# Two pairs of first-layer tiles by seven products on the half blocks, laced with plain tiles

## The chip, the cores and the metric

The kernel runs on one NeuronCore of a Trainium2 chip. The metric is the device time of one execution in microseconds; 655.01 us is the median of three runs before the change. One of the executions was taken by the hardware profiler, and all profile lines come from that one.

The engines named below are PE (TensorE, matrix products; PEld is its weight load), DVE (VectorE), ACT (ScalarE), POOL (GpSimd) and SP (SyncE, which here only issues DMAs). Each works through its own queue in order. PE writes to PSUM[...].

## The reference

A gated linear attention over 768 steps with complex gates, for 32 heads of 48 channels, followed by a two-layer network with the gate h cos(h):

```python
for t in range(S):
    ar, ai = (a_re_n[:, :, t, :, None], a_im_n[:, :, t, :, None])
    new_re = ar * S_re - ai * S_im
    new_im = ar * S_im + ai * S_re
    kv = np.einsum('bhd,bhe->bhde', k[:, :, t], v[:, :, t])
    S_re, S_im = (new_re + kv, new_im)
    y[:, :, t] = np.einsum('bhd,bhde->bhe', q[:, :, t], S_re)
...
h = x @ w_in
g = h * np.cos(h)
return (g @ w_out).astype(np.float32)
```

`x` has 3072 rows (tokens) of 384; `w_in` is 384 x 2048 and `w_out` 2048 x 384. All is fp32.

## The kernel before

The 3072 tokens are cut into 24 chunks of 128, and two chunks make a group: 12 groups, 0 to 11. For each group the kernel computes the logs and phases of the gates (`log_steps`, `p_powers` with PSUM tile `lgs`, `g_phase` with `phs`), scales keys and queries by them (`g_stack`: tiles `ks`, `qs`), turns both (`f_transpose`: a DVE transpose into tile `tr`, a DMA to a buffer `moved` in DRAM, DMAs back as `kT` and `qT`), multiplies scores (`sc`, masked by DVE into `atm`), adds values and the carried state (`yp`, `sp`), and sends the result through DRAM into `xT` (`f_x`, `f_xt`), the transposed input of the network.

The first layer takes `xT`, 3 blocks of 128 channels x 2 chunks of 128 tokens. It makes the 2048 hidden columns in 8 tiles jp = 0 to 7 of 256 columns each. One tile fills one PSUM bank `hp` with 2 x 3 products of 128 weight columns and 256 tokens (`mm1_sums`, line 1061). Then ACT writes the cosine to `gate` and squares `hp` into a scratch tile with a running sum (`gate_sine`), and DVE multiplies (`gate_product`). A product in fp32 leaves two matmul records in the profile, each with its weight load.

The second layer of groups 2 to 11 already works by seven products instead of eight on half blocks: `mixed` (line 1140) forms sums and differences of gate tiles in tiles `s`, `quarters` and `last_quarter` those of `w_out`, and `seventh` multiplies them into the tiles `sum` and `op`.

Groups 0, 1 and the first steps of 2 are ordered by hand. From group 2 on, a loop at line 1568 laces the work. Pass n holds the second layer of group n-1, the attention of group n, the gates and keys of group n+1, and from 0.56 of its length the first layer of group n (`first`). The function `weave` (line 1213) sorts the pieces by the fractions written beside them. The products on PE are chained in just that order. On DVE, ACT and SP the framework's scheduler lays the pieces out by what is ready; each engine then keeps that order. Every operation of DVE and many of ACT are recorded at line 676, all products at 687, so tiles tell them apart.

The parts of a pass that matter here, in PE's order: scores and values of group n, among them second-layer products of group n-1; the `lgs` products for group n+1; more second-layer products; the `phs` products; the last 16 records of the second layer; then the whole first layer. `keys(n+1)` (trigonometry, `g_stack`, `p_end`, both `f_transpose`) runs on DVE and ACT at the start of that first layer. `p_end` reads the tile `end`, the last row of P, which `even_steps` sends out and back through DRAM (`row_out`, `row_back`, lines 833 and 838).

PSUM is split into two pools: `pa`, five banks under one name for attention work, and `pm`, three banks for `hp`, `op` and `sum`.

```python
              (phases(n + 1), *((0.472, 0.476) if n == PLAIN else (0.516, 0.524))),
              (keys(n + 1), *((0.5, 0.62) if n == PLAIN else (0.53, 0.64))),
              (last_quarter() if n == PLAIN else [], 0.9, 1.0), (first(n), 0.56, 1.0),
```

Of the kernel before, what the change touches and what calls it, by code (L numbers as in the profile page):

```python
# [11 lines left out]
F32 = mybir.dt.float32  # L12
# [475 lines left out]
def fast_path(ctx, tc, q, k, v, a_re, a_im, moe_w_in, moe_w_out, out, least, odd, wide,  # L488
# [323 lines left out]
    def even_steps(g, i, n):  # L812
# [16 lines left out]
        if g > 0:  # L829
            row_out(g, i, n, nc.sync)  # L830
            row_back(g, i, n, nc.sync)

    def row_out(g, i, n, queue):
        P = cut(X[g]["P"], i, n)
        queue.dma_start(out=X[g]["row"][ds(i * DM, n * DM)],
                        in_=P[C - 1:C].rearrange("o x -> (o x)"))
# [215 lines left out]
    def f_xt(g, i=0, n=G):  # L1052

        if i == 0:
            X[g]["xT"] = msb.tile([C, ND, G, C], F32, tag="xT", name="xT")
        moved = X[g]["moved"].rearrange("p s d g t -> (p s d) g t").rearrange("(c r) g t -> r c g t", r=C)
        put = nc.sync.dma_start(out=X[g]["xT"][:, :, ds(i, n)], in_=moved[:, :, ds(i, n)])
        behind(put, late["x"])
        late["x"] = put
# [18 lines left out]

    def gate_sine(g, jp):
        x = X[g]  # L1080
        ps = x["hp"][jp]
        gate = x["gate"][jp] = msb.tile([C, 2, G * C], F32, tag="gate", name="gate", bufs=8)
        junk = msb.tile([C, 2, G * C], BF16, tag="junk", name="junk", bufs=1)
        special(out=gate, in_=ps, func=AF.Sin, scale=1.0 / in_scale, bias=half_pi_b)
# [3 lines left out]
    def gate_product(g, jp):  # L1088
        x = X[g]
        gate = x["gate"][jp]  # L1090
        gated = vector.tensor_tensor(out=gate, in0=x["hp"].pop(jp), in1=gate, op=ALU.mult)
        x.setdefault("gated", gated)

    def mm1_gate(g, jp):
        gate_sine(g, jp)
        gate_product(g, jp)

# [4 lines left out]
    def mm2(g, i, j0, nj):  # L1102
# [7 lines left out]
        if j0 + nj == NJ:  # L1110
            ot = msb.tile([C, DM], F32, tag="ot", name="ot")
            scalar.mul(out=ot, in_=ps, mul=1.0 / (in_scale * out_scale))
            nc.sync.dma_start(out=out[ts(g * G + i, C), :], in_=ot)
# [26 lines left out]
    def mixed(g, p):  # L1140
# [3 lines left out]
        s = stage["pool"].tile([C, 3, 2, C], F32, tag="s", name="s", bufs=HJ // 2)  # L1144
        s1, s2, s4 = (s[:, i] for i in range(3))
# [14 lines left out]
    def seventh(g, p, part):  # L1160
# [34 lines left out]
        elif p == 4:  # L1195
            put = nc.sync.dma_start(out=out[ds(row + C, C), :], in_=x["ot"][1])
            if g == NG - 1:
                behind(put, late["read SP"])
# [61 lines left out]
    def chunks(g):  # L1260
# [6 lines left out]
        if g + 2 < NG:  # L1267
            yield lambda: load(g + 2, ("k", "q", "v"))

    def first(g):  # L1270
        order = range(NJ // 2) if g < PLAIN else (0, 4, 1, 5, 2, 6, 3, 7)
# [296 lines left out]
    for n in range(2, NG):  # L1568
        weave((mixes(n - 1, 2, 4), 0.0, 0.12), (logs(n + 1), 0.0, 0.02), (chunks(n), 0.0, 0.36),
              (upper[2:] if n == 2 else [], 0.0, 0.2), (products(n - 1, 0, 2 + (n < NG - 1)), 0.0, 0.36),  # L1570
              (prods(n + 1), 0.25, 0.27), (second(n - 1, 1), 0.36, 0.5),
              (products(n - 1, 2 + (n < NG - 1), 7), 0.4, 0.56),
              (phases(n + 1), *((0.472, 0.476) if n == PLAIN else (0.516, 0.524))),
              (keys(n + 1), *((0.5, 0.62) if n == PLAIN else (0.53, 0.64))),
              (last_quarter() if n == PLAIN else [], 0.9, 1.0), (first(n), 0.56, 1.0),
# [102 lines left out]
```

## Time and profile before

| | |
|---|---|
| median of three runs | 655.01 us (654.78 to 655.53) |
| the profiled execution | 653.01 us |
| its span, first to last instruction | 651.2 us |
| matmul records, PE | 4075 |
| of them `hp` of 256 columns | 1128, 246.5 us |
| of them `hp` of 128 columns | 48, 6.0 us |
| ACT `gate<-hp` and DVE `gate<-hp`, each | 96 x 0.69 us |
| DVE transposes `tr<-ks` and `tr<-qs` | 20 x 2.25 us |
| first layer of one group, from first to last `hp` | 20.72 us |

The first layers of groups 3 to 11, the ones that the change touches, start at 204.16, 255.37, 305.61, 355.93, 407.14, 457.37, 507.69, 559.38 and 607.45 us. The page names the time by engines and groups of instructions; a stage is best read from the windows view (busy time of each engine between two moments) with the timelines of the engines beside it. Matmuls overlap in their records: the mean of one `hp` record is 379 ns, but the next starts 216 ns after it. Start-to-start is the price; the rest is drain.

### The profile page before, as it was taken

Reading aid. Unit: us, or ns where it says so; the run is one execution under the profiler, and the core shown is the slowest. Engines: PE = TensorE matmul, PEld = TensorE weight load, DVE = VectorE, ACT = ScalarE, POOL = GpSimd, SP = SyncE. Lnnn points to the kernel's source line nnn. Section 1 sums busy time; section 2 is a strip of 40 time slices with the busy share of each in tenths; the row PEclk is TensorE's granted clock in tenths of the full one; section 3 lists DMA queues with packets and bytes.
Section 4 is the critical chain, followed back from the end, with each engine's and each line's share of the span. In section 5 each row is a group of like instructions: output and inputs, shape, how many; then the busy total and the mean of one; then the engine's idle time right before and its main releaser. Section 6 shows DMA issues by size and latency. Waiting matters only on the chain.

```text
span 651.2 us, 10758 instructions
## 1 busy us (share of the span) xinstructions
PE 641.0 (98%) x4075; PEld 576.4 (89%) x4075; DVE 492.0 (76%) x799; ACT 392.8 (60%) x726; POOL 30.9 (5%) x53
## 2 busy tenths in 40 slices
PE   8999999999999999999999999999999999999997
PEld 6888877777999999899899899899899999999996
DVE  6999989888687688786787787876877878862251
ACT  7898687284583593494494485485576476433330
POOL 4010200000000000010010010000000000000000
PEclk9999999999999999999999999999999999999999
DMA  9968755727627656747738737836836843363001
GB/s 249 244 179 203 225 164 123 170 62 182 146 49 182 158 146 148 194 110 167 209 82 191 204 85 167 205 96 151 226 105 146 219 123 98 112 134 120 25 1 31
DMA packets 232920, 94.90 MB, mean 146 GB/s; under 512 B 208701, under 2 KB 221246, under 8 KB 232858
## 3 DMA queue, kind: packets, MB, share of 16 engines
q1 hardware_dynamic: 225320, 68.51, 45.3%
q0 software_dynamic: 5824, 25.50, 11.7%
q8 instruction: 34, 0.56, 0.4%
q10 hardware_dynamic: 1714, 0.11, 0.2%
q14 instruction: 28, 0.23, 0.1%
HBM read 69.28 MB, written 24.81 MB: 144 GB/s over the span
## 4 chain that ended last, share of the span: by engine, by line
PE 92%; ACT 4%; DVE 3%; DMA 0%; issue 0%; SPq 0%; DVEq 0%
PE hp L687 38%; PE op L687 18%; PE sum L687 16%; PE sc L687 6%; PE yp L687 6%; PE sp L687 4%; PE phs L687 2%; PE lgs L687 1%; ACT tan L707 1%; PE yr L687 1%; PE tp L948 1%; ACT rs L707 1%; ACT lg L707 1%; ACT L703 1%; DVE mag L676 1%; DVE atm L676 1%
## 5 line engine op out<-in xcount | busy, mean ns | idle before, releaser
L687 PE MATMUL hp<-xT,w_in 128*128 128x256 f32 (+1 forms) x1176 | 252.5, 375 | 0.0
L687 PEld LDWEIGHTS hp<-xT,w_in 128*128 128x128 f32 x1176 | 219.6, 190 | 30.2 <-issue 0.2
L707 ACT ACTIVATE gate<-hp,half_pi_b 128x512 f32<-128x512 f32 x96 | 66.0, 687 | 118.5 <-PE hp L687 118.5
L687 PE MATMUL op<-w_out,gate 128*128 128x192 f32 (+1 forms) x448 | 100.7, 374 | 0.0
L676 DVE TENSOR_TENSOR gate<-hp,gate 128x512 f32<-128x512 f32 x96 | 65.7, 684 | 45.8 <-ACT junk L676 45.7
L687 PEld LDWEIGHTS op<-w_out,gate 128*128 128x128 f32 x448 | 75.9, 190 | 16.9 <-issue 2.0
L676 ACT ACTIVATE junk<-hp 128x512 bf16<-128x512 f32 x96 | 56.7, 591 | 0.0
L687 PE MATMUL sum<-t_s,s 128*128 128x192 f32 x320 | 56.3, 329 | 0.0
L687 PEld LDWEIGHTS sum<-t_s,s 128*128 128x128 f32 x320 | 52.1, 190 | 1.5 <-issue 1.5
L676 DVE TENSOR_TENSOR atm<-sc,causal 128x512 f32<-128x512 f32 x48 | 32.9, 689 | 23.4 <-PE sc L687 23.4
L687 PEld LDWEIGHTS sc<-qT,kT 96*128 96x128 f32 x384 | 47.4, 192 | 2.3 <-issue 0.6
L687 PE MATMUL sc<-qT,kT 96*128 96x128 f32 x384 | 49.0, 276 | 0.2 <-ACT qT L676 0.2
L676 ACT ACTIVATE ot<-sum 128x192 f32<-128x192 f32 x39 | 12.6, 322 | 53.7 <-PE sum L687 53.4
L676 DVE SCALAR_TENSOR_TENSOR ot<-op,ot 128x192 f32<-128x192 f32 x40 | 13.3, 354 | 38.0 <-PE op L687 36.4
L687 PE MATMUL yp<-atm,v 128*48 128x128 f32 x352 | 33.6, 277 | 0.9 <-ACT Q L707 0.6
L703 ACT ACT_TABLE_LOAD x24 | 30.8, 1283 | 1.2 <-PEq L1662 0.7
L676 ACT COPY yT<-yp 48x512 f32<-48x512 f32 x44 | 25.3, 574 | 7.4 <-PE yp L687 7.0
L687 PE MATMUL yp<-qT,state 96*48 96x128 f32 x304 | 29.7, 272 | 0.0
L687 PE MATMUL sum<-w_out,gate 128*128 128x192 f32 x160 | 29.7, 329 | 0.0
L687 PE MATMUL sp<-v,ks 128*96 128x48 f32 x320 | 29.7, 245 | 0.0
L687 PEld LDWEIGHTS sp<-v,ks 128*96 128x96 f32 x320 | 29.6, 165 | 0.0
L676 ACT CAST tan<-phs 128x384 int32<-128x384 f32 x24 | 11.4, 480 | 29.4 <-PE phs L687 29.4
(147 smaller groups left out, 987.4 us busy)
## 6 DMA issues: line engine op xcount, KB each, us to landing
moved<-tr SPq DMA_DIRECT2D x20, 768.0 KB
raw<-in_moe_w_in_dram POOLq DMA_DIRECT2D x16, 768.0 KB, 5.1
raw<-in_moe_w_out_dram POOLq DMA_DIRECT2D x16, 768.0 KB, 4.6
kT<-moved SPq DMA_DIRECT2D x40, 192.0 KB
qT<-moved SPq DMA_DIRECT2D x10, 768.0 KB
k<-in_k_dram SPq DMA_DIRECT2D x24, 192.0 KB
q<-in_q_dram SPq DMA_DIRECT2D x24, 192.0 KB
v<-in_v_dram SPq DMA_DIRECT2D x24, 192.0 KB
```

The costliest lines, as they stand in the source:

```text
L676: ins = getattr(self.engine, op)(**kw)
L687: chain(nc.tensor.matmul(out, **kw), "tensor")
L703: chain(nc.scalar.preload_act_table_set(table))
L707: chain(nc.scalar.activation(func=func, **kw))
L948: chain(nc.tensor.transpose(ps[:, h], X[g][name[0] + "s"][:, x0 + h].rearrange("p a d -> p (a d)"), ident), "tensor")
```

## The change

It changes four of the eight tiles of the first layer in groups 3 to 11. Tiles jp and jp+4 with jp = 0 and jp = 2 form a pair; the two tiles, two chunks of tokens and the first two of the three channel blocks make a 2 x 2 by 2 x 2 block product, done by seven products on mixed blocks; the third channel block is added plainly. Counted in matmul records, a pair takes 44 records of 128 tokens (22 products with 128 weight columns each) instead of 24 records of 256 tokens (12 products).

- `halves_mixed` forms the mixed weights once (three new blocks of 256 columns for each pair, and one in place in `w_in`), on DVE; `x_mixed` forms five mixed blocks of `xT` for each group, on DVE.
- `in_sevens(g, b, step)` does one pair in four steps. Both tiles of the pair live in banks of pool `pa`, two regions of 256 columns in each: "11" and "12" in the upper tile's bank, "21" and "22" in the lower one's. Region "12" carries the running sum; it is copied three times by ACT into the gate tiles (`kept`), and DVE adds the copies into the other regions.
- `first` runs the pairs' steps with the plain tiles 1, 5, 3, 7 between them.
- The mixed gates `s` of the second layer get no tiles of their own but buffers of `qs` and `tr`.
- The write of the last row of P and its two reads (`ends`) become a piece of their own at 0.36 of the pass, and on SP they, the loads of k, q, v and the stores of the output stand behind the write of `xT`.

On PE the 96 records of a group's first layer become 136. Nothing else on PE moves.

```diff
--- before.py
+++ after.py
@@ -826,14 +826,19 @@
         for one_, what in zip(ins, ("carried", "split")):
             if what in x and g > PEG:
                 behind(one_, x[what])
-        if g > 0:
-            row_out(g, i, n, nc.sync)
-            row_back(g, i, n, nc.sync)
+        if 0 < g <= PLAIN:
+            ends(g)
+
+    def ends(g):
+        put = row_out(g, 0, G, nc.sync)
+        if g > PLAIN:
+            behind(put, X[g - 1]["back"])
+        row_back(g, 0, G, nc.sync)
 
     def row_out(g, i, n, queue):
         P = cut(X[g]["P"], i, n)
-        queue.dma_start(out=X[g]["row"][ds(i * DM, n * DM)],
-                        in_=P[C - 1:C].rearrange("o x -> (o x)"))
+        return queue.dma_start(out=X[g]["row"][ds(i * DM, n * DM)],
+                               in_=P[C - 1:C].rearrange("o x -> (o x)"))
 
     def row_back(g, i, n, queue):
         row = X[g]["row"][ds(i * DM, n * DM)]
@@ -1056,7 +1061,7 @@
         moved = X[g]["moved"].rearrange("p s d g t -> (p s d) g t").rearrange("(c r) g t -> r c g t", r=C)
         put = nc.sync.dma_start(out=X[g]["xT"][:, :, ds(i, n)], in_=moved[:, :, ds(i, n)])
         behind(put, late["x"])
-        late["x"] = put
+        late["x"] = X[g]["back"] = put
 
     def mm1_sums(g, jp, i=None):
 
@@ -1076,24 +1081,111 @@
                        rhs=x["xT"][:, dc, ds(lo, n)].rearrange("p g t -> p (g t)"),
                        start=(dc == 0), stop=(dc == ND - 1))
 
+    def alike(*tiles):
+
+        if len(tiles[-1].shape) == 3:
+            return tiles
+        return [t.rearrange("p j (i c) -> p j i c", i=G) for t in tiles[:-1]] + [
+            tiles[-1].rearrange("p i j c -> p j i c")]
+
     def gate_sine(g, jp):
         x = X[g]
         ps = x["hp"][jp]
-        gate = x["gate"][jp] = msb.tile([C, 2, G * C], F32, tag="gate", name="gate", bufs=8)
+        if jp not in x["gate"]:
+            x["gate"][jp] = msb.tile([C, 2, G * C], F32, tag="gate", name="gate", bufs=8)
+        gate = x["gate"][jp]
         junk = msb.tile([C, 2, G * C], BF16, tag="junk", name="junk", bufs=1)
+        gate, junk, ps = alike(gate, junk, ps)
         special(out=gate, in_=ps, func=AF.Sin, scale=1.0 / in_scale, bias=half_pi_b)
         scalar.activation(out=junk, in_=ps, func=AF.Square, scale=1.0 / in_scale,
                           accum_out=wide[:, ds(g * (NJ // 2) + jp, 1)])
 
     def gate_product(g, jp):
         x = X[g]
-        gate = x["gate"][jp]
-        gated = vector.tensor_tensor(out=gate, in0=x["hp"].pop(jp), in1=gate, op=ALU.mult)
+        gate, ps = alike(x["gate"][jp], x["hp"].pop(jp))
+        gated = vector.tensor_tensor(out=gate, in0=ps, in1=gate, op=ALU.mult)
         x.setdefault("gated", gated)
 
     def mm1_gate(g, jp):
         gate_sine(g, jp)
         gate_product(g, jp)
+
+    SEVENS, PARTED = 3, (0, 2)
+    parted = {}
+
+    def halves_mixed():
+
+        for b in PARTED:
+            t = parted[b] = stage["pool"].tile([C, 3, W], F32, name=f"w_mix{b}")
+            a11, a12, a21, a22 = (w_in[:, r * (NJ // 4) + b, c] for r in range(2) for c in range(2))
+            yield lambda t=t, a=a21, b_=a22: vector.scalar_tensor_tensor(
+                out=t[:, 0], in0=a, scalar=-1.0, in1=b_, op0=ALU.mult, op1=ALU.subtract)
+            yield lambda t=t, a=a11: vector.scalar_tensor_tensor(
+                out=t[:, 1], in0=t[:, 0], scalar=-1.0, in1=a, op0=ALU.mult, op1=ALU.subtract)
+            yield lambda t=t, a=a12: vector.tensor_tensor(
+                out=t[:, 2], in0=a, in1=t[:, 1], op=ALU.subtract)
+            yield lambda a=a11, b_=a21: vector.tensor_tensor(out=b_, in0=a, in1=b_, op=ALU.subtract)
+
+    def x_mixed(g):
+
+        xT = X[g]["xT"]
+        t = X[g]["xm"] = stage["pool"].tile([C, 5, C], F32, tag="xm", name="xm", bufs=1)
+        b12, b21, b22 = xT[:, 0, 1], xT[:, 1, 0], xT[:, 1, 1]
+        vector.tensor_tensor(out=t[:, 0:2], in0=xT[:, 0::2, 0], in1=xT[:, 0::2, 1], op=ALU.subtract)
+        vector.tensor_tensor(out=t[:, 2], in0=b22, in1=t[:, 0], op=ALU.add)
+        vector.tensor_tensor(out=t[:, 3], in0=b22, in1=b12, op=ALU.subtract)
+        vector.tensor_tensor(out=t[:, 4], in0=b21, in1=t[:, 2], op=ALU.subtract)
+
+    def in_sevens(g, b, step):
+
+        x, up, low = X[g], b, b + NJ // 4
+        if step == 0:
+            for jp in up, low:
+                x.setdefault("hp", {})[jp] = pa.tile([C, G, 2, C], F32, tag="a", name="hp")
+                x.setdefault("gate", {})[jp] = msb.tile([C, 2, G * C], F32, tag="gate",
+                                                        name="gate", bufs=8)
+        xT, xm, mix = x["xT"], x["xm"], parted[b]
+        place = {"11": (up, 0), "12": (up, 1), "21": (low, 0), "22": (low, 1)}
+
+        def at(c):
+            jp, i = place[c]
+            return x["hp"][jp][:, i]
+
+        def kept(c):
+            jp, i = place[c]
+            return x["gate"][jp][:, :, ds(i * C, C)]
+
+        def product(c, a, moving, fresh=False):
+            for ji in range(2):
+                matmul(at(c)[:, ji], lhsT=a[:, ts(ji, C)], rhs=moving,
+                       start=fresh and ji == 0, stop=True, skip_group_check=True)
+
+        def add(c, a):
+            vector.tensor_tensor(out=at(c), in0=at(a), in1=kept(c), op=ALU.add)
+
+        if step == 0:
+            product("12", w_in[:, up, 0], xT[:, 0, 0], True)
+            scalar.copy(out=kept("11"), in_=at("12"))
+            product("11", w_in[:, up, 1], xT[:, 1, 0])
+            product("11", w_in[:, up, 2], xT[:, 2, 0])
+            add("11", "11")
+        elif step == 1:
+            product("12", mix[:, 1], xm[:, 2])
+            scalar.copy(out=kept("21"), in_=at("12"))
+            product("21", w_in[:, low, 0], xm[:, 3], True)
+            product("21", w_in[:, low, 2], xT[:, 2, 1])
+        elif step == 2:
+            product("12", mix[:, 0], xm[:, 0])
+            scalar.copy(out=kept("22"), in_=at("12"))
+            add("22", "21")
+        else:
+            product("12", mix[:, 2], xT[:, 1, 1])
+            product("12", w_in[:, up, 2], xT[:, 2, 1])
+            mm1_gate(g, up)
+            product("21", w_in[:, low, 1], xm[:, 4])
+            product("21", w_in[:, low, 2], xm[:, 1])
+            add("21", "21")
+            mm1_gate(g, low)
 
     def mm1(g, jp):
         mm1_sums(g, jp)
@@ -1110,7 +1202,9 @@
         if j0 + nj == NJ:
             ot = msb.tile([C, DM], F32, tag="ot", name="ot")
             scalar.mul(out=ot, in_=ps, mul=1.0 / (in_scale * out_scale))
-            nc.sync.dma_start(out=out[ts(g * G + i, C), :], in_=ot)
+            put = nc.sync.dma_start(out=out[ts(g * G + i, C), :], in_=ot)
+            if g > 0 and i > 0:
+                behind(put, X[g + 1]["back"])
 
 
 
@@ -1141,8 +1235,10 @@
 
         lo, hi = X[g]["gate"][p], X[g]["gate"][p + HJ // 2]
         a11, a21, a12, a22 = lo[:, :, 0:C], lo[:, :, C:2 * C], hi[:, :, 0:C], hi[:, :, C:2 * C]
-        s = stage["pool"].tile([C, 3, 2, C], F32, tag="s", name="s", bufs=HJ // 2)
-        s1, s2, s4 = (s[:, i] for i in range(3))
+        if p % 2 == 0:
+            pool, tag = ((gt, "qs"), (ft, "tr"))[p // 2]
+            X[g]["s"] = pool.tile([C, 2, 3, 2, C], F32, tag=tag, name="s")
+        s1, s2, s4 = (X[g]["s"][:, p % 2, i] for i in range(3))
         for out_, a, b, op in ((s1, a21, a22, ALU.add), (s2, s1, a11, ALU.subtract),
                                (a21, a11, a21, ALU.subtract), (s4, a12, s2, ALU.subtract)):
             vector.tensor_tensor(out=out_, in0=a, in1=b, op=op)
@@ -1194,8 +1290,7 @@
             behind(nc.sync.dma_start(out=out[ds(row, C), 0:E2], in_=c11), late["line"])
         elif p == 4:
             put = nc.sync.dma_start(out=out[ds(row + C, C), :], in_=x["ot"][1])
-            if g == NG - 1:
-                behind(put, late["read SP"])
+            behind(put, late["read SP"] if g == NG - 1 else X[g + 1]["back"])
         elif p == 6 and alone:
             late["store"] = lambda: nc.scalar.dma_start(out=out[ds(row, C), E2:DM], in_=c12)
         elif p == 6:
@@ -1265,9 +1360,15 @@
             yield lambda n=n: f_out(n)
         yield lambda: (f_x(g), f_xt(g))
         if g + 2 < NG:
-            yield lambda: load(g + 2, ("k", "q", "v"))
+            yield lambda: load(g + 2, ("k", "q", "v"), put=lambda **kw: behind(
+                nc.sync.dma_start(**kw), X[g]["back"]))
 
     def first(g):
+        if g >= SEVENS:
+            plan = [(0, 0), 1, (0, 1), (2, 0), 5, (0, 2), (2, 1), 3, (0, 3), (2, 2), 7, (2, 3)]
+            return [lambda: x_mixed(g)] + [
+                (lambda it=it: in_sevens(g, *it)) if isinstance(it, tuple) else (lambda it=it: mm1(g, it))
+                for it in plan]
         order = range(NJ // 2) if g < PLAIN else (0, 4, 1, 5, 2, 6, 3, 7)
         return [lambda jp=jp: mm1(g, jp) for jp in order]
 
@@ -1568,10 +1669,12 @@
     for n in range(2, NG):
         weave((mixes(n - 1, 2, 4), 0.0, 0.12), (logs(n + 1), 0.0, 0.02), (chunks(n), 0.0, 0.36),
               (upper[2:] if n == 2 else [], 0.0, 0.2), (products(n - 1, 0, 2 + (n < NG - 1)), 0.0, 0.36),
-              (prods(n + 1), 0.25, 0.27), (second(n - 1, 1), 0.36, 0.5),
+              (prods(n + 1), 0.25, 0.27),
+              ([lambda: ends(n + 1)] if n + 1 < NG else [], 0.36, 0.37), (second(n - 1, 1), 0.36, 0.5),
               (products(n - 1, 2 + (n < NG - 1), 7), 0.4, 0.56),
               (phases(n + 1), *((0.472, 0.476) if n == PLAIN else (0.516, 0.524))),
               (keys(n + 1), *((0.5, 0.62) if n == PLAIN else (0.53, 0.64))),
+              (halves_mixed() if n == SEVENS else [], 0.1, 0.4),
               (last_quarter() if n == PLAIN else [], 0.9, 1.0), (first(n), 0.56, 1.0),
               (mixes(n, 0, 2), 0.9, 1.0), (guarded(n - 1, per) if n > 3 else [], 0.1, 0.9))
     checked = verdict(late, temp)
```

## The prediction

> **What bounds the kernel now.** I read the page's busy table first, then the windows over one first-layer stage, then the timelines of PE, DVE and ACT inside it, and last the chain of waits. The page says that TensorE is the limit and is never slowed:
>
> ```profile
> span 651.2 us, 10758 instructions
> PE 641.0 (98%) x4075; PEld 576.4 (89%) x4075; DVE 492.0 (76%) x799; ACT 392.8 (60%) x726; POOL 30.9 (5%) x53
> ...
> PEclk9999999999999999999999999999999999999999
> ```
>
> Windows over a group's first layer, its remaining work, and the next first layer:
>
> ```profile
> 407.14:427.86 20.72, 20.72 (x98) 18.24 (x98) 16.70 (x27) 9.45 (x23) 0.00 (x0) 1.00 0.76 193
> 427.86:457.37 29.51, 29.36 (x235) 28.21 (x234) 21.95 (x35) 22.25 (x37) 1.78 (x3) 1.00 0.51 127
> 457.37:478.09 20.72, 20.72 (x98) 18.25 (x97) 16.72 (x27) 9.46 (x23) 0.00 (x0) 1.00 0.79 202
> ```
>
> The first layer takes 20.72 us with PE busy for all of it: 96 records (each fp32 product is recorded twice) at 0.216 us. Nothing PE does there waits for anybody, because each result bank is filled in one go and read afterwards. What DVE does in that time is no part of the path, and it is a lot. The timeline of DVE from the start of the stage at 457.37 (I call it T0):
>
> ```profile
> 458.70 0.95 DVE L676 TENSOR_TENSOR qs<-mag,rs 128x768 f32<-128x768 f32 x1
> 459.57 0.95 DVE L676 TENSOR_TENSOR qs<-mag,lo 128x768 f32<-128x768 f32 x1
> 460.43 0.17 DVE L676 TENSOR_SCALAR end<-end 96x16 f32<-96x16 f32 x1
> 460.51 2.26 DVE L676 STREAM_TRANSPOSE tr<-ks 128x1536 f32<-128x1536 f32 x1
> 462.69 0.14 DVE L676 SCALAR_TENSOR_TENSOR least<-end,least 96x16 f32<-96x16 f32 x1
> 462.74 0.69 DVE L676 TENSOR_TENSOR gate<-hp,gate 128x512 f32<-128x512 f32 x1
> 463.34 2.25 DVE L676 STREAM_TRANSPOSE tr<-qs 128x1536 f32<-128x1536 f32 x1
> 465.51 0.66 DVE L676 TENSOR_TENSOR gate<-hp,gate 128x512 f32<-128x512 f32 x1
> ```
>
> DVE is still on the next group's keys until T0+3.06, and then has two transposes of 2.2 us. The first gate product, ready early, is taken only at T0+5.4, and nobody minds. Two rows of PE's timeline give the price of a narrow product:
>
> ```profile
> 41.65 2.84 PE L687 MATMUL hp<-xT,w_in 128*128 128x128 f32 x24
> ...
> 427.86 1.06 PE L687 MATMUL sc<-qT,kT 96*128 96x128 f32 x8
> 428.75 1.47 PE L687 MATMUL sum<-w_out,gate 128*128 128x192 f32 x8
> ```
>
> The eight 128-wide records start 0.89 us before what follows them: 0.111 us each. The 24 records of the first layer's own tiles take 2.84 us with a last drain of some 0.17 us: also 0.111 to 0.112. So the weight load does not hold a 128-wide product back. Outside the stage there is one tight spot, in the chain of waits after a stage that ended at 427.86:
>
> ```profile
> 438.12 0.69 DVE atm L676
> 438.81 0.86 DVE mag L676
> 439.68 0.88 DVE lo L676
> 440.56 0.04 issue
> 440.60 0.80 PE lgs L687 x3
> ```
>
> PE's `lgs` products wait there for DVE's `lo`.
>
> [...] at 60.43 a product started 0.056 us after DVE's `ks`, PE having stood 0.42 us. [...]
>
> **The change part by part.** *Products.* In each of groups 3 to 11, tiles 0, 4, 2, 6 lose 48 records of 256 columns and get 88 of 128 (2 pairs x 22 products x 2 records). 48 x 0.216 = 10.36 us become 88 x 0.112 = 9.86: 0.50 us saved per group, if PE never waits. That is the whole gain, 4.5 us in nine groups.
>
> *New waits, A.* The order of the built program shows each pair's first step as two products into region 12, an ACT copy of it, and products into region 11 of the same bank, the first of which waits for that copy[...]. Behind it on PE stands everything. At T0 four records take 0.45 us; the last starts at 0.336, ends by the profile at 0.61 (mean 278 ns), ACT starts 0.03 later. A copy of 128x256 is not in the trace; `ot` rows of 192 and 384 columns (322 and 486 ns) give 377 ns by line. Then 0.055 us as above: PE resumes at 1.08 instead of 0.45, idle 0.63. If ACT is late it is more; ACT's `ot` ends at T0+0.59 (457.65 plus 0.31), just in time. The second pair's first step costs the same, 0.63: its copy stands behind tile 1's gate and another copy, both over by then. Bounds for each: 0.5 (a 0.25 us copy) to 1.0.
>
> *New waits, B.* Step 1 puts products into region 12 of the first pair's bank again and so waits for DVE's add into region 11. DVE's order in the built program of groups 3 to 9: `qs` (to T0+3.06), three `xm` mixes, transpose of ks, the fourth mix, that add, transpose of qs. Durations: a 256-wide elementwise starts the next after 0.34 us (rows of `s`), a 128-wide one after about 0.21 (768-wide: 0.87, by line). 3.06 + 0.34 + 0.21 + 0.21 = 3.82; transpose 2.18 gives 6.00; mix 6.21; add of 0.42 ends at 6.63; PE can go at 6.68. PE itself arrives after 1.08 + 8 x 0.112 + 12 x 0.216 = 4.56. Idle 2.12 us. Bounds: 1.2 (mixes for nothing, as in group 10) to 3. In group 10 the mixes stand ahead of the keys, in DVE's old gap (3.59 us idle at 555.94), so the add ends at 3.06 + 2.18 + 0.42 = 5.66 and PE idles 1.16. Group 11 has no keys to turn: no B.
>
> *The other waits in the stage.* Carrying the same durations on: the second pair's add is ready at 10.6 (DVE free of the second transpose at 8.8), PE needs it at 13.0; copies of region 12 follow gates of 1.26 us on ACT and are done at 14.4, 14.7 and 20.1, needed at 17.0, 18.8 and 21.8; adds into 22 are done at 15.0 and 20.7, needed at 17.9 and 22.7. All hidden. The stage takes 20.72 - 0.50 + 0.63 + 2.12 + 0.63 = 23.60 us in groups 3 to 9.
>
> *After the stage.* The last pair's two gates, 2 and 6, now both come at the end, behind gate 7: ACT leaves the stage at +2.2 us after its end instead of +1.35, and DVE has two adds and more mixes there. The next log chain starts 0.83 us later, and DVE loses the 0.94 us that it idled before `atm` (438.12). I get the end of `lo` at +13.3 instead of +12.7. `lgs` wants it at +12.3, +12.9 or +13.8, as the chunks fall: before, it came 0.45 late in three of seven groups, in time in the others. Extra: 3 x 0.6 + 2 x 0.4 = 2.6 us, between 0 and 6.
>
> *At nothing.* The mixing of w_in: six of eight 256-wide operations (some 2.5 us) stand in the built program before the `atm` at 127.47, where DVE idled 2.23 us for scores; the rest before the idle 0.84 us of the next `atm`; without that cover PE would lose the 2.5. `s` in the homes of qs and tr: its last readers among the products, 16 records before T0, end before `qs` is written (first half at about T0-1.3 against T0+1.33), and the `moved` write that frees tr is out before `s` starts. Row and end on SP: the row write goes behind xT, k, q and v, the two 3 KB reads between both `moved` writes; `end` is wanted by DVE only after the second pair's add (T0+10.6 or later), some 3 us after it is issued; the qs write and the kT and qT reads issued behind it move by about 1.3 us of issue plus DVE's 0.7, and the qT read was issued at 420.75 for scores at 427.86. The stores put behind xT wait on nothing that PE needs.
>
> *Sum.* Seven groups x (2.12 + 1.26 - 0.50) = 20.2; group 10: 1.92; group 11: 0.76; after stages 2.6: 25.4 us. The profiled execution took 653.01 (span 651.2 and 1.8 around it), so 678.4 for such a run; the median of the runs is 2.0 above it: 680.4.
>
> **The rivals.** (1) Waits at A stay but B mostly goes (add sooner, waits under 1 us): 680.4 - 7 x 1.3 = 671. For it: the mixes are estimated; against: the transpose alone is 2.2 us and stands ahead. (2) More late work after the stage: scores' `atm` has some 0.2 us of slack before `yp`, and ACT comes late to A: 1 us per group more, 689. For it: DVE runs without a gap there; against: the slack holds by my count. (3) Faster: DVE and ACT keep ahead of PE in this stage, the place being the first step of each pair. It decides when the three waits together are under 0.50 us in a group; with none, 655.0 - 4.5 = 650.5. For it: DVE has 4 us free in the stage (16.72 of 20.72 busy). Against it: the idle time is at the end, and A alone is 1.26, since a copy cannot start before its products end. (4) The pauses lower PE's clock. [...] the trace never has such a pause in this loop and holds full clock. [...]
>
> **How the numbers follow.** Forecast 0.62, 671 to 686 on its own; rival 1 0.15; rival 2 0.14; rival 3 0.04; rival 4 0.03; the remaining 0.02 spreads. The range is 670 to 690, which takes in both neighbours and most of the bounds of B. A measurement tells 0.2% (1.3 us) from no change: faster 0.04, within 0.01, slower 0.95.
>
> **What would show it.** In the profile after: stages of some 23.6 us from first to last `hp`; PE's waits led by `hp` on DVE `hp` (about 15 us) and on ACT `gate` (about 11 us); 128-wide `hp` at 0.112 us a record; PE's share near 95%. A stage of 20.2 us with no such waits would refute A and B; waits placed at the second transpose, at `end` or at `sc` would mean that I have the queue wrong.

## The result and the profile after

The changed kernel takes 686.42 us (median of four, 686.18 to 689.72) against 655.27 us of the kernel before in the same job: a ratio of 1.049, interval 1.0462 to 1.0517, or 31.1 us more. The forecast was 680.4 us with a range of 670 to 690; the sign and the range hold, the sum of 25.4 us fell 5.7 short.

The page of the changed kernel first, the lines that answer to those of before. PE is busy 4 us longer in all, but its share falls from 98% to 94%, and the clock line still shows nothing but nines up to the last slice:

```profile
span 684.7 us, 11658 instructions
...
PE 644.9 (94%) x4435; PEld 582.1 (85%) x4435; DVE 518.1 (76%) x897; ACT 406.8 (59%) x780; POOL 29.5 (4%) x53
...
PEclk9999999999999999999999999999999999999998
```

So the time is lost to waiting. The list of PE's waits (engine, what it wanted, line, who released it, us in total, times, longest) says on whom. In the kernel before it has no entry for `hp` or `lgs`, and 0.3 us for `yp` on `atm`:

```profile
PE hp L687 <- DVE hp L676: 13.5, 8, 1.9
PE hp L687 <- ACT gate L676: 8.9, 18, 0.6
PE yp L687 <- DVE atm L676: 4.3, 9, 1.1
...
PE lgs L687 <- DVE lo L676: 1.2, 2, 0.7
```

The first two are waits B and A of the prediction. The other two lie after the stages; of the 4.3 us of `yp`, 0.9 stand ahead of the first changed stage, and stand there in the kernel before too (0.6 of them under ACT). As the profile puts it, no idle time between the stages is a wait for a bank of `pa`, of whose five the pairs now take four. Windows over a stage, the rest of a pass and the next stage (length first, then busy time of PE, PEld, DVE, ACT, POOL, clock, DMA share, GB/s):

```profile
367.14:390.87 23.73, 20.98 (x137) 19.01 (x137) 16.93 (x31) 10.20 (x27) 0.00 (x0) 1.00 0.64 157
390.87:421.86 30.99, 30.90 (x253) 29.51 (x251) 25.98 (x45) 23.19 (x40) 1.71 (x3) 1.00 0.57 137
421.86:445.60 23.74, 20.98 (x138) 19.01 (x137) 16.91 (x31) 10.20 (x27) 0.00 (x0) 1.00 0.65 157
```

The stage took 20.72 us before and takes 23.7 to 24.0 now in groups 3 to 9 (22.9 in group 10, 21.7 in group 11), with PE busy for 21.0 of it. The timeline of PE at the start of the stage at 530.94 (start, duration, then what ran; in brackets the idle time before it):

```profile
530.94 0.61 PE L687 MATMUL hp<-xT,w_in 128*128 128x128 f32 x4
532.01 3.75 PE L687 MATMUL hp<-xT,w_in 128*128 128x128 f32 x20 [0.46 <-ACT gate L676]
537.52 0.71 PE L687 MATMUL hp<-xm,w_mix 128*128 128x128 f32 x4 [1.76 <-DVE hp L676]
...
540.09 3.75 PE L687 MATMUL hp<-xT,w_in 128*128 128x128 f32 x20 [0.52 <-ACT gate L676]
```

These are A, B and the second A. Beside the second and third row stand, on ACT and DVE, the copy and the queue that hold PE:

```profile
531.58 0.37 ACT L676 COPY gate<-hp 128x256 f32<-128x256 f32 x1
```

```profile
533.13 0.95 DVE L676 TENSOR_TENSOR qs<-mag,lo 128x768 f32<-128x768 f32 x1
534.00 0.62 DVE L676 TENSOR_TENSOR xm<-xT 128x256 f32<-128x256 f32 x2
534.53 0.29 DVE L676 TENSOR_TENSOR xm<-xT,xm 128x128 f32<-128x128 f32 x1
534.73 2.22 DVE L676 STREAM_TRANSPOSE tr<-ks 128x1536 f32<-128x1536 f32 x1
536.87 0.26 DVE L676 TENSOR_TENSOR xm<-xT,xm 128x128 f32<-128x128 f32 x1
537.04 0.43 DVE L676 TENSOR_TENSOR hp<-hp,gate 128x256 f32<-128x256 f32 x1
```

The copy ends at 531.95 and PE goes on at 532.01; the add ends at 537.47 and PE goes on at 537.52. Both releases are 0.05 to 0.06 us.

Where the time of the two profiled executions went:

| stretch | before | after | more | predicted |
|---|---|---|---|---|
| to the first stage by sevens | 204.2 | 204.4 | 0.3 | 0 |
| nine stages, groups 3 to 11 | 186.5 | 210.9 | 24.3 | 22.8 |
| eight stretches between them | 237.5 | 244.0 | 6.6 | 2.6 |
| after the last stage | 23.1 | 25.4 | 2.3 | 0 |

The last row is mostly one transfer: PE's last record comes 0.5 us later after its stage, and the rest is the last store, which ended 6.0 us after its issue against 4.2. The two executions differ by 33.5 us; the medians differ by 31.1, about the first three rows. So the stages are 1.5 us dearer than predicted and the stretches between them 4.2 (with the 0.3). That second sum is the open question; the first experiments test A and B, the next ones look for it.

### The profile page after: what moved, and what is told of

The parts are those of the page before. It is cut to its first block, busy times and chain, and to the rows that moved or that the text cites. A ratio compares the mean times of both kernels' runs of the same rounds, so it can differ in the third digit from the quotient of the medians.

```text
span 684.7 us, 11658 instructions
## 1 busy us (share of the span) xinstructions
PE 644.9 (94%) x4435; PEld 582.1 (85%) x4435; DVE 518.1 (76%) x897; ACT 406.8 (59%) x780; POOL 29.5 (4%) x53
## 4 chain that ended last, share of the span: by engine, by line
PE 72%; ACT 14%; DVE 6%; issue 3%; DMA 3%; ACTq 0%; SPq 0%; DVEq 0%
PE hp L687 34%; PE op L687 14%; PE sum L687 11%; PE yp L687 3%; PE sc L687 3%; PE phs L687 2%; PE sp L687 2%; ACT rs L707 2%; ACT junk L676 2%; ACT tan L707 2%; DMA raw<-in_moe_w_in_dram 2%; ACT L703 1%; DMA raw<-in_moe_w_out_dram 1%; ACT gate L707 1%; DVE tan L676 1%
## 5 line engine op out<-in xcount | busy, mean ns | idle before, releaser
L687 PE MATMUL hp<-xT,w_in 128*128 128x256 f32 (+1 forms) x1104 | 211.6, 343 | 8.9 <-ACT gate L676 8.9
L687 PEld LDWEIGHTS hp<-xT,w_in 128*128 128x128 f32 x1104 | 178.5, 191 | 30.0 <-ACT gate L676 12.3
L676 DVE SCALAR_TENSOR_TENSOR ot<-op,ot 128x192 f32<-128x192 f32 x40 | 13.3, 353 | 30.0 <-PE op L687 30.0
L676 DVE TENSOR_TENSOR hp<-hp,gate 128x256 f32<-128x256 f32 x54 | 23.0, 425 | 14.8 <-PE hp L687 14.8
L687 PE MATMUL hp<-xm,w_mix 128*128 128x128 f32 x144 | 21.3, 281 | 13.5 <-DVE hp L676 13.5
L687 PEld LDWEIGHTS hp<-xm,w_mix 128*128 128x128 f32 x144 | 19.0, 191 | 17.2 <-DVE hp L676 16.7
L676 ACT COPY gate<-hp 128x256 f32<-128x256 f32 x54 | 19.3, 378 | 18.0 <-PE hp L687 17.5
```

What stands on the lines that cost most here:

```text
L676: ins = getattr(self.engine, op)(**kw)
L687: chain(nc.tensor.matmul(out, **kw), "tensor")
```

## The experiments

Each kernel ran beside the kernel before on the same chip; times are medians, and the ratio is to the kernel before in that job (655.45 to 655.88 us).

**e1, wait B alone taken away.** DVE's transposes are put behind the first add:

```diff
+        if "added" in X[g - 1]:
+            behind(turn, X[g - 1]["added"])
...
-            vector.tensor_tensor(out=at(c), in0=at(a), in1=kept(c), op=ALU.add)
+            x.setdefault("added", vector.tensor_tensor(out=at(c), in0=at(a), in1=kept(c), op=ALU.add))
```

The pieces of `keys` also get a later place in the pass, so that the transposes come after the add in program order.

> The changed kernel with DVE's order altered: both transposes of the next group's keys and queries are put behind the first add into region 11, so that step 1 of the first pair finds its bank free. The copies that step 0 waits for (wait A) stay. My theory: wait B goes (2.03 us idle in each of seven groups, 1.19 in group 10), 686.4 - 15.4 = 671. The stage is then 21.7 us instead of 23.7. Rival: the stage is long because the narrow products or the mixes hold PE, or another wait comes up right behind B; then 682 to 687.

Measured: 669.4 us, ratio 1.0213 (1.0188 to 1.0237). The stages are 21.7 us, but three of them end with up to 1.1 us in which the scores wait for qT, since the transposes moved too. PE's list has no wait on DVE's `hp` left:

```profile
PE hp L687 <- ACT gate L676: 8.9, 18, 0.6
PE yp L687 <- DVE atm L676: 3.3, 8, 0.8
PE sc L687 <- DMA qT<-moved: 1.7, 3, 1.1
```

B is what DVE's order makes of it, and it is worth its full length: the stages without a late qT are 2.03 us shorter than 23.72, the 1.92 us that PE stood and 0.10 that the first record after a wait costs (worked out below). Of the 17.2 us between the two profiled executions, 13.3 lie in the stages; 2.3 lie between them and 1.4 after the last, so B's order also cost something after the stage. `lgs` no longer waits there.

**e2, the first wait A alone taken away.** Tile 1 goes between the copy and the products that wait for it; that the transpose of qs follows the add is now written down, and the pieces of `keys` get a later place to allow it:

```diff
-            plan = [(0, 0), 1, (0, 1), (2, 0), 5, (0, 2), (2, 1), 3, (0, 3), (2, 2), 7, (2, 3)]
+            plan = [(0, "0a"), 1, (0, "0b"), (0, 1), (2, 0), 5, (0, 2), (2, 1), 3, (0, 3), (2, 2), 7, (2, 3)]
```

> The changed kernel with tile 1 moved between the two halves of the first pair's step 0, so that the copy of region 12 has 2.6 us of plain products to hide behind; the transpose of ks still stands ahead of the add on DVE. My theory: the first wait A is worth nothing where B follows, since B's end is set by DVE's queue (T0+6.6) and not by PE's arrival; PE comes 0.6 earlier and waits 0.6 longer. In four groups the product of gate 1 now slips ahead of that add, +0.63 each; only group 11, which has no B, gains 0.63: 686.4 + 2.5 - 0.6 = 688.3. Rival: the waits add up, each removed one is gained in full: 686.4 - 9 x 0.63 = 680.7.

Measured: 698.8 us, ratio 1.0686 (1.0626 to 1.0747), well above what either theory gave, with four executions from 695.8 to 704.4. The stages say why. In group 3 the stage is 23.66 us, as in the changed kernel (23.68): the A that was removed came back in B, as expected. In group 4 it is 24.31, the gate product ahead of the add. But groups 5, 6 and 8 took 28.9, 27.3 and 27.3 us. Windows of three of these stages (the granted clock is the number before the DMA share):

```profile
258.95:283.26 24.31, 20.71 (x138) 19.10 (x137) 17.02 (x31) 10.21 (x27) 0.00 (x0) 1.00 0.64 154
312.77:341.68 28.91, 24.74 (x138) 22.62 (x137) 17.71 (x32) 11.28 (x28) 0.00 (x0) 0.82 0.58 139
372.66:399.95 27.29, 23.70 (x138) 21.65 (x137) 16.88 (x31) 10.22 (x27) 0.00 (x0) 0.87 0.56 138
```

and the timeline of PE behind the wait of the second one:

```profile
320.51 1.22 PE L687 MATMUL hp<-xm,w_mix 128*128 128x128 f32 x4 [3.65 <-DVE hp L676]
...
324.81 6.05 PE L687 MATMUL hp<-xT,w_in 128*128 128x128 f32 x20 [0.52 <-ACT gate L676]
```

20 records take 6.05 us where the same 20 take 3.75 above. Behind this pause the granted clock was 0.50 over 320.51 to 324.51 and 324.51 to 328.51; behind the one of 3.08 us in group 6 it was 0.50 over 383.31 to 387.41, and behind that of group 8 eight records took 1.76 us in place of 1.06; behind that of group 4 it stayed at 1.00. This was rival 4 of the prediction. Taking away a short wait in front of a long one made the long one longer (3.08 us in group 4 against 1.77 in the changed kernel), and in three groups PE was slower behind it. These three stages lie 5.2, 3.0 and 3.0 us above the 23.7, 24.3 and 24.3 that were expected of them, 11 us together; 698.8 lies 10.5 above the expected 688.3. In group 5 not all of it is the clock: DVE's keys begin 1.2 us later against PE than in group 3, so the pause itself is 1.2 us longer.

**e4, the side edits without the sevens.** `SEVENS, PARTED = NG, (0, 2)`: no group by sevens, everything else of the change kept (the mixing of w_in goes with the sevens).

> The changed kernel with no group by sevens: what is left is the moved row and end traffic on SP, the order of stores and loads behind xT, the mixed gates in the homes of qs and tr, and the mixing of w_in is left out with the sevens. My theory: nothing that PE waits for moves, 655 (within 1.5 us). Rival: the order on SP or the shared homes delay the attention after each stage and are the source of the 4 us that I missed: 658 to 662.

Measured: 662.5 us, ratio 1.0109 (1.0084 to 1.0135): 6.9 us for edits that I had put at nothing. The stages are 20.72 us as before but for one (21.25); the time lies between them, and one entry leads PE's list (0.9 us of it ahead of these stages, as in the kernel before):

```profile
PE yp L687 <- DVE atm L676: 8.6, 11, 1.7
```

DVE's timeline shows what stands ahead of `atm`; first for the first chunk, after a stage that ended at 328.52, then for the second, after one that ended at 433.33:

```profile
334.61 0.96 DVE L676 SCALAR_TENSOR_TENSOR mag<-re,mag 128x768 f32<-128x768 f32 x1 [0.84 <-ACT mag L707]
335.48 0.55 DVE L676 TENSOR_SCALAR lg<-lg 128x768 f32<-128x768 f32 x1
335.95 0.69 DVE L676 TENSOR_TENSOR atm<-sc,causal 128x512 f32<-128x512 f32 x1
```

```profile
443.43 0.96 DVE L676 TENSOR_TENSOR mag<-mag,tan 128x768 f32<-128x768 f32 x1 [0.30 <-ACT tan L707]
444.30 0.95 DVE L676 SCALAR_TENSOR_TENSOR lo<-lg,hi 128x768 fp32r<-128x768 f32 x1
445.17 0.95 DVE L676 SCALAR_TENSOR_TENSOR tan<-mag,tan 128x768 f32<-128x768 f32 x1
446.04 0.68 DVE L676 TENSOR_TENSOR atm<-sc,causal 128x512 f32<-128x512 f32 x1
```

In the kernel before, `atm` came first in both places (330.17 against `mag` at 332.41; 438.12 against `mag`, `lo`, `tan` from 438.73). The first kind is the dear one: five waits of 0.7 to 1.7 us, 6.3 together; the second makes four waits and 1.4 us. The edits say nothing of these operations. They move DMAs on SP; the scheduler, which lays the work out by what it takes to be ready, now lays the log chain of the next group ahead of the mask, and PE's `yp` waits. That it takes the scores to be later is a guess from its manner of working, the changed order is seen.

**e5, e9, e10: which side edit.** The kernel before with one of them each: the mixed gates in the homes of qs and tr; the row and end at 0.36 of the pass behind xT; the loads and stores behind xT.

> The kernel before with one of the side edits: the mixed gates s take the homes of qs and tr; DMA order on SP as before. Theory now: the 7 us of the side edits come from the order on SP, which makes the scheduler lay the log chain ahead of atm on DVE; the homes cost nothing: 655 (within 1.5). Rival: the homes hold up the mixes or the transposes: 658 to 662.

> The kernel before with only the row of P and its two reads moved to 0.36 of the pass, behind the write of xT. In DVE's order the log chain's mag, lo and tan now stand ahead of the second chunk's atm, the first chunk's atm stays early. Theory: yp of the second chunk waits some 0.4 and 0.3 us in each stage, and 655.4 + 9 x 0.35 = 658.5. Rival: this edit is free and the stores do all of it: 655.

> The kernel before with only the loads of k, q, v and the stores of the output put behind the write of xT. In DVE's order atm of both chunks now stands behind gates, mixes and the log chain. Theory: the waits of 1.1 to 1.7 us for the first chunk's atm come from here, 660. Rival: free, 655.

Measured: e5 655.5 us, ratio 1.0005 (0.9987 to 1.0023), so the homes are free within 0.2%. e9 658.4, ratio 1.0046 (1.0028 to 1.0063); e10 659.3, ratio 1.0052 (1.0035 to 1.0069). 2.84 and 3.72 us make 6.6, near the 6.9 of e4, but that is chance: the long waits for the first chunk's `atm`, 6.3 us in e4, stand in neither trace, so they come only with both edits together. The size of e9 was right and its reason mostly wrong: `yp` waits only 1.6 us there, while the scores stand 3.5 us in three stages; the profile puts 0.7 of that down to qT and the rest to nobody. SP's timeline in one of these stages makes qT likely for all:

```profile
263.14 0.33 SPq L938 DMA_DIRECT2D moved<-tr  x1
263.56 1.50 SPq L847 DMA_DIRECT2D end<-row  x2
265.87 0.34 SPq L938 DMA_DIRECT2D moved<-tr  x1
...
272.72 0.78 SPq L943 DMA_DIRECT2D qT<-moved  x1
```

The reads of `end` stand between the two writes of the transposes, and the read of qT goes out 15.2 us after this stage's start (257.56), against 13.7 in the same group before. It isn't the issue alone: in group 9 the read goes out at 15.0 us in both kernels, and the scores stand 0.1 us before and 0.9 in e9. e10 has the expected wait on `atm`, but shorter (0.4 us at most), 1.1 us for xT and 0.7 for qT.

**e6, the change with the SP edits undone.** The row and end, loads and stores as in the kernel before; sevens and homes kept.

> The changed kernel, sevens and homes kept, with the SP edits undone: row and end, the loads of k, q, v and the stores stand where they stood before. Theory: the stage stays at 23.7 us, the time from a stage's end to the next falls back to 29.6 to 30.5, and the late products yp with it: 686.4 - 6.9 = 679.5. Rival: in the changed kernel the late work comes from gates 2 and 6 at the end of the stage, not from SP: 684 to 686.

Measured: 698.6 us, ratio 1.0629 (1.0579 to 1.068): neither. PE's waits:

```profile
PE hp L687 <- DVE hp L676: 15.7, 7, 4.2
PE hp L687 <- ACT gate L676: 11.3, 18, 1.9
PE hp L687 <- DMA xT<-x: 4.9, 4, 1.6
PE lgs L687 <- DVE lo L676: 1.6, 4, 0.4
```

The waits of `yp` are gone but for the 0.9 us of before, so in the changed kernel too they came with the SP edits. Those of `lgs` for `lo` stay (1.6 us against 0.4 before), so they need no SP edits. The stretches between the stages are no shorter for it, 7.3 us more than before: xT is late now, and the first copy with it. In two groups the add falls behind both transposes, PE pauses for 4.2 us and runs slower after it (20 records took 6.06 us in place of 3.75; the mean clock of this execution is 0.982): two stages of 30.7 us. The SP edits pay for something: they bring xT in time, which the kernel before did without them. Neither theory had seen that.

**e3, e7, e8: all waits of the stage covered.** The plan laces both pairs so that a plain tile or the other pair stands between each copy or add and the products that want it, and the transposes stand behind the first add:

```diff
+            plan = [(0, "0a"), 1, (0, "0b"), (2, "0a"), 5, (0, 1), (2, "0b"), (0, 2), 3, (2, 1),
+                    (0, "3a"), (2, 2), (0, "3b"), (2, 3), 7]
```

e7 is e3 with the SP edits undone and the mixing of the gates begun at 0.93 of the pass in place of 0.9, so the two differ by more than SP; e8 is e7 with an order by hand on DVE (the log chain, cut into pieces for it, has its `mag` operations behind `atm`). In e3 the mixed gates of a lower tile are formed before that tile's gate is written, from what its buffer held; the durations are those of the same operations.

> All three waits covered: each pair's step 0 is cut in two with a plain tile or the other pair's half between copy and the next products, step 3 is cut likewise, and both transposes stand behind the first add. My theory: the stage falls to 20.7 - 0.5 = 20.2 us; the time is 655.3 - 4.5 plus whatever of the late work after the stage (6.6 us in the changed kernel, where gates 2 and 6 come last) remains: 651 to 657. Rival: the late work comes from the mixes and adds that fill DVE, not from the order of the tiles; then the full 6.6 stays and it is 657 or more. If the narrow products cost more than 0.112 us a record next to others, the stage will be over 20.7.

> The laced order of e3 (all waits in the stage covered but one of 0.28 us, transposes behind the first add) with the SP edits undone, so that the two writes of the transposes and the reads of kT follow each other on SP without the 2.2 us of the end reads between them; the mixes of the gates start at 0.93 of the pass in place of 0.9. Theory: the wait of sc for qT (9.0 us over nine groups in e3) all but goes, 672.8 - 9 = 664, less what the SP edits cost after the stage; its DVE order still has the log chain ahead of atm, so 657 to 664. Rival: qT is late because the transposes are, the end reads don't matter: 670 to 673.

> As e7, and the log chain of the next group is put behind the atm operations on DVE by hand (the mag operations behind the second atm of the first chunk and the first atm of the second). Theory: the waits of yp for atm go (some 4 us), 655.3 - 4.5 + 2.5 (the wait of 0.28 us in nine stages) = 653, up to 657 if qT is still late in some. Rival: lgs then waits for lo instead, and the time stays as in e7.

Measured: e3 672.8 us, ratio 1.0259 (1.0234 to 1.0284); e7 665.8, 1.015 (1.0116 to 1.0184); e8 667.3, 1.0162 (1.0122 to 1.0202). In all three the waits A and B are gone from the stage but for one of 0.28 us (foreseen from e7 on), and what follows the stage is late instead; e3 lies far above its 651 to 657, on the side of the rival ("657 or more") but not for the rival's reason. In e3, at the end of the stage at 467.34:

```profile
490.53 1.28 PE L687 MATMUL sc<-qT,kT 96*128 96x128 f32 x8 [2.29 <-DMA qT<-moved]
```

The scores wait for qT, 9.0 us in six stages: both transposes had stepped behind the add, and the reads of `end` stood between their writes. The two longest of these waits are 2.29 and 1.99 us; the mean granted clock of this execution is 0.993, against 1.000 in the kernel before. Without these reads e7 still waits 5.3 us for qT, and 2.6 for `atm`; so `atm` can be late without the SP edits too. In e8 the waits for `atm` are gone as expected, so their cause is DVE's order; but now xT is late, 6.2 us of waits in six places. e7 comes to 1.8 us above the expected range, e8 to 10.3.

**e11, e12: every cause found so far removed at once.** On DVE the transpose of ks first, then mixes, add, transpose of qs, and the gate of tile 1 behind the add; the upper tile's gate behind the copy that the last step wants; row and end behind the transposes on SP; loads and stores behind xT as in the change; the log chain behind `atm`. e12 also puts the second store behind xT:

```diff
-            nc.sync.dma_start(out=out[ds(row, C), :], in_=x["ot"][0])
+            put = nc.sync.dma_start(out=out[ds(row, C), :], in_=x["ot"][0])
+            if g < NG - 1:
+                behind(put, X[g + 1]["back"])
```

> All causes found so far taken away at once, sevens kept: the laced order of e3; on DVE the transpose of ks first, then the mixes, the first add, the transpose of qs, and only then the gate of tile 1; the gate of the upper tile behind the copy for the last step; row and end behind the transposes on SP; the loads and stores behind xT as in the change; the log chain behind atm as in e8. Theory: stages of 20.2 us, no wait for qT, atm or xT, so 655.3 - 4.5 = 651. Rival: with DVE and ACT this full another late piece takes over after the stage and the gain of 0.5 us per group is lost: 655 to 660.

> As e11, and the second store of the output is also put behind the read of xT on SP, where in e11 it stood between the write of x and the read of xT, waited for its result and held that read (42.5 us of waits of hp for xT). Theory: with that gone the stages are 20.2 us as in the last group of e11, nothing else is late, 655.4 - 4.5 = 651 (649 to 654). Rival: qT, atm or lo take over after the stage, 655 to 660.

Measured: e11 716.7 us, ratio 1.0926 (1.0899 to 1.0953); e12 669.9, 1.022 (1.0196 to 1.0243). e11 shows what one DMA in the wrong place costs. SP's timeline for the group that starts at 453.05:

```profile
437.90 0.89 SPq L1059 DMA_DIRECT2D x<-yT  x2
448.80 0.36 SPq L1307 DMA_DIRECT2D out_dram<-ot  x1
449.61 0.38 SPq L1068 DMA_DIRECT2D xT<-x  x1
```

The store waits 10 us for its result and holds the read of xT behind it. PE waits 42.5 us for xT in all, 32.1 of it in seven groups behind such a store. The stage at 453.05 then takes 22.94 us with PE busy throughout, at a mean clock of 0.88; over the whole execution the clock is 0.96. With that store moved, e12 has the stage that was aimed at, and almost nothing late after it. Windows over a stage and the last group's stage:

```profile
420.50:441.07 20.57, 20.35 (x137) 18.79 (x137) 17.03 (x30) 11.38 (x30) 0.00 (x0) 1.00 0.71 184
...
624.04:644.23 20.19, 20.19 (x138) 18.95 (x137) 8.30 (x19) 10.94 (x28) 0.00 (x0) 1.00 0.03 11
```

The last group, which has no keys of a next one to turn, takes 20.19 us: 0.53 less than before, the whole of what seven products can give here. The other eight end with 0.6 to 2.8 us from the start of the last `hp` to the scores, where the last group has 0.2 to what follows; of this the profile puts 2.8 us down to qT and 2.9 to nobody; the read of qT goes out 14.4 us after the stage's start against 13.6 before (medians), and two of them have a remainder of B. Against nine stages of 20.19 that is 8.5 us, more than the 4.8 that the sevens saved. The stretches between stages are 0.65 us longer in all than before, not 6.6. The rest of e12's excess is a wait of 10.4 us for xT in group 2's stage, which has no sevens; the mean clock of this execution is 0.990, against 1.000 in the kernel before. e11 has the same wait. SP's timeline there shows whose it is:

```profile
145.47 1.90 SPq L1059 DMA_DIRECT2D x<-yT  x2
158.55 0.34 SPq L944 DMA_DIRECT2D moved<-tr  x1
159.06 0.38 SPq L1068 DMA_DIRECT2D xT<-x  x1
```

The write of the next group's first transpose stands ahead of the read of xT, and that transpose ends on DVE at 158.53. No run puts this order right. No version with sevens in this study beats the kernel before.

## Why the prediction was right, and where it was short

The measured 686.4 lies just beyond the 671 to 686 that the forecast claimed for itself, on the way to the 689 of rival 2; the range held because it took in that rival. The two large terms, A and B, are right in mechanism; the term after the stage is not.

*Products.* Right: 0.50 us saved per group was predicted, 0.53 seen in e12, at 0.112 us a record.

*A.* Right in place and size: 0.63 predicted, 0.62 and 0.68 by starts (the gap between two starts less one record), with one of 0.75.

*B.* Right: DVE's queue sets it, PE was to go at T0+6.68 and goes at 6.58. Counted by starts, PE stands 1.92 us against 2.12, because it came 0.10 us later and went on 0.10 earlier; in group 10, 1.08 against 1.16. e1 shows it by itself.

*The stage.* 23.72 against 23.60. That this is so near owes something to luck, since B was 0.20 too long and another term was missing: the first narrow record after each wait is followed by the next only 0.213 us later, not 0.112. Three waits make 0.30 us. The sum closes: 20.72 - 0.53 + 0.62 + 1.92 + 0.68 + 0.31 = 23.72. In nine stages this and the small differences make the 1.5 us.

*After the stage.* This step failed: 2.6 us predicted with bounds 0 and 6, 6.6 measured, and mostly by another wait. It made `lgs` wait for `lo` in five groups. `lgs` waits in two, 1.2 us against 0.4 before. What I left out is the wait of `yp` for `atm`, 3.4 us in these groups, which rival 2 named and I dismissed with "the slack holds by my count". It held in the kernel before, whose DVE order I read. In the changed one 1.8 us of it stand behind `mag`, `lo` and `tan` (I followed the built order only up to the end of `lo`), and 1.6 for the first chunk behind the mixes of the gates. In group 9 the longest of each, 1.1 us for `atm` and 0.7 for `lo`, also have DVE standing 0.69 and 1.17 us ahead of them for weights read into the tile `raw`; the kernel before has no such pause there. Together this is 4.2 us more idle time; the rest I take to be what idle time leaves out, since by starts a wait costs more (A is 0.46 idle and 0.62 by starts; nine waits at some 0.2 make about 2, an estimate).

*At nothing.* The homes are free (e5) as predicted, and the mixing of w_in is within the 0.3 us of the table's first row. The row, end and stores on SP are not: 6.9 us alone (e4). I had counted their issue time on SP and asked whether data comes too late, and found 1.3 us of issue with room behind it. The cost came by another way, the order that a scheduler gives another engine. That gates 2 and 6 come last does not make `lgs` late by itself: they are last in e1 too, where it has no such wait. What share of the late work is theirs is not separated by any run.

*Rivals.* The clock (rival 4) did not move in the stages of the profiled execution of the changed kernel: it is 1.00 up to 680.28 us, with a longest pause in the loop of 1.89 us. In e7 a pause of 1.98 us was followed by a clock of 0.50. B was forecast at 2.12 us, above that, so rival 4 was put too low. The one execution of 689.7 us, at a mean clock of 0.994 against 0.997 to 0.999, may be a case of it; it has no trace. Rival 3 needed waits under 0.50 us in a group: group 11 of e11 has that, and groups 3, 7 and 11 of e12, whose stages are shorter than 20.72 us.

## What to carry to other kernels

Fewer products help only if each partial result is wanted later than copy, add and queue can give it (here they saved 0.53 us a stage, and A and B cost 3.22): count what the accumulation reads back between products, and lace other work there before counting what is saved. After any edit to DMA order under a scheduler, read the order of every engine again as if it had been edited, since the cost here (6.9 us in e4) was in an engine that the edit does not mention. A wait removed in front of a longer one is not a gain, and can be a loss; in e7 a pause of PE of 1.98 us cost about another 1.7 (an estimate: half of the 3.41 us that followed it at a clock of 0.50).

## What the hardware showed beyond the expected

Pauses and PE's clock. In e7, around a wait for qT, PE stood 1.98 of 3.41 us; in the next 3.41 us the granted clock was 0.50, and in the 3.41 after these 1.00. In e2, around a B of 2.48 us in group 9, PE stood 1.95 of 3.41 us and 1.05 of the next 3.41 (the rest of B and the second A, of 0.52), and the clock stayed at 1.00. The windows of e7, then of e2:

```profile
485.23:488.64 3.41, 1.43 (x11) 1.26 (x11) 3.29 (x9) 3.39 (x8) 0.75 (x2) 1.00 0.25 61
488.64:492.05 3.41, 3.41 (x15) 3.41 (x14) 2.29 (x5) 3.37 (x4) 0.19 (x1) 0.50 0.74 223
492.05:495.46 3.41, 3.41 (x35) 3.19 (x36) 3.03 (x5) 2.38 (x4) 0.00 (x0) 1.00 0.04 12
```

```profile
544.60:548.01 3.41, 1.46 (x11) 1.22 (x9) 3.41 (x6) 1.27 (x3) 0.00 (x0) 1.00 0.00 0
548.01:551.42 3.41, 2.36 (x18) 2.17 (x19) 3.22 (x4) 0.75 (x2) 0.00 (x0) 1.00 0.81 232
```

Pauses behind which a clock or a pace was read:

| run | PE stood, us | waiting for | behind it |
|---|---|---|---|
| e6, at 323.79 | 4.17 | B | 20 records in 6.06 us (3.75 in the changed kernel) |
| e2, group 5 | 3.65 | B | clock 0.50 in two windows of 4.00 us, 0.87 in the third |
| e2, group 6 | 3.08 | B | clock 0.63, then 0.50 for 4.10 us, then 0.98 |
| e2, group 8 | 3.08 | B | 8 records in 1.76 us (1.06 in group 4) |
| e2, group 4 | 3.08 | B | clock 1.00 over the stage |
| e2, groups 7 and 9 | 2.48 | B | clock 1.00 |
| e7, before 488.64 | 1.98 | qT | clock 0.50 for 3.41 us |
| e8, at 310.56 | 1.98 | xT | mean clock of the execution 0.999 |
| after, groups 3 to 10 | 0.92 to 1.89 | B | clock 1.00 |

So the length of a pause alone does not decide: 3.08 us in group 4 of e2 left the clock at 1.00, and 1.98 in e7 did not. What else decides was not shown. At a clock of 0.50, in group 5 of e2, four 128-wide records took 0.86 us from start to start (321.52 to 322.38) where four took 0.45 in group 4 (266.67 to 267.12).

The second surprise is the 0.10 us that the first narrow record of `hp` loses after a wait at full clock. In the stages of the changed kernel, in an unbroken row, the weight load of a record starts 0.109 us ahead of it, and the next record starts 0.112 us after it (medians). After each of the 26 waits of `hp` the load starts with the record, 0.001 to 0.002 us ahead, and the next record starts 0.213 to 0.214 us later. That the load's late start is what costs the 0.10 us is likely from these starts, an estimate: no run was made to test it.
